# A gated recurrence and its feed-forward layer: 64-token chunks, k and b stacked, one solve pass, the feed-forward steps interleaved by a list scheduler

## The chip, the cores and the metric

One core of one Trainium2 chip runs the kernel, in one launch. The metric is device time in microseconds (us). A run that is over 1.5% above the fastest of its own kernel is called slow here, and only fast runs are compared. The engines have these names in the profile: PE is TensorE (matmul), PEld its weight load, DVE is VectorE, ACT is ScalarE, POOL is GpSimd, SP is SyncE, whose queue issues most of the DMAs (SPq). SBUF is the core's working memory; PSUM is the memory that TensorE writes its results to, in a few buffers.

## The reference

Four batches, eight heads, 768 tokens, 40 features a head. Each head carries a 40 x 40 state through the tokens; the result goes through a layer with squared relu.

```python
for t in range(S):                                   # 768 tokens
    y[:, :, t] = einsum('bhd,bhde->bhe', r_t, state) # read before the update
    Sa = einsum('bhde,bhe->bhd', state, a_t)
    state = state * w_t[:, :, None, :] - Sa (x) b_t + v_t (x) k_t
x = y.transpose(0, 2, 1, 3).reshape(3072, 320)
h = maximum(x @ w_in, 0)                             # 320 x 2048
out = (h * h) @ w_out                                # 2048 x 320, fp32
```

## The kernel before

It works in chunks of 128 tokens, six of them, for all 32 heads; a quad is four heads that lie in the same half of the array's rows. Decay is taken as cumulated logarithms (fp32 matmuls with a triangle of ones), k and b are divided by the decay and a and r multiplied by it. Then come triangular products within the chunk and products with the carried state. After all chunks the feed-forward layer (FFN) runs by itself.

```python
L = 128
# emit_prep, once per chunk: cumulated decay, fp32
cs = ps_prep_f32("cs")
nc.tensor.matmul(out=cs[:, 0:n], lhsT=UTI[:], rhs=lnW[:, s0:s1], start=True, stop=True)
# ... the same with UTE; the last row's decay spread to all rows, fp32 (rep)
rep = ps_prep_f32("rep")
nc.tensor.matmul(out=rep[:, 0:8 * D], lhsT=SEL127[:], rhs=GAM[:, c0:c0 + 8 * D], start=True, stop=True)
# ... transposes of R, V, K, A (bf16) and of the decay (fp32, trw)

# stage2, once per quad; stage1 has made the triangles Em and CmT
for i in range(4):
    nc.tensor.matmul(out=mstp[:, i, :], lhsT=AT[pb:pb + D, prs[i], :],      # 40 rows of the array
                     rhs=ST2[pb:pb + D, prs[i], :], start=True, stop=False)
    nc.tensor.matmul(out=mstp[:, i, :], lhsT=Em[:, i, :],                   # 128 rows
                     rhs=Vp[:, hhs[i], 0:D], start=False, stop=True)
# ...
for i in range(4):
    nc.tensor.matmul(out=xtp[:, i, :], lhsT=AT[pb:pb + D, prs[i], :],
                     rhs=Zb[pb:pb + D, i, :], start=True, stop=False)
    nc.tensor.matmul(out=xtp[:, i, :], lhsT=Em[:, i, :],
                     rhs=CmT[:, i, :], start=False, stop=True)
# ... yp (output), stp (state), stx (its transpose)

# after each chunk: 32 small copies by DMA that turn the heads' outputs into columns of x
nc.sync.dma_start(out=XTg[g][row0:row0 + D, tok0:tok0 + L], in_=YS[pb:pb + D, pr, :])

# after all chunks: the FFN
for j in range(16):                                    # in a loop over blocks tb of 512 tokens
    for g in range(3):
        nc.tensor.matmul(out=hp[:], lhsT=WIN[g][:, j * 128:(j + 1) * 128],
                         rhs=XTg[g][:, tb * 512:(tb + 1) * 512], start=(g == 0), stop=(g == 2))
    # ... copy to SBUF, max(x, 0) * x, then 16 matmuls of 320 columns with WOUT
```

Of the kernel before, what the change touches and what calls it, by code (L numbers as in the profile page):

```python
# [7 lines left out]
FP32 = mybir.dt.float32  # L9
BF16 = mybir.dt.bfloat16  # L10
ALU = mybir.AluOpType
ACTF = mybir.ActivationFunctionType


@with_exitstack
def kernel(
# [13 lines left out]

    NB, NHH, T, D = r.shape
    NH = NB * NHH
    L = 128
    NCH = T // L
    NP = NH // 2
    NQ = NH // 4
    DFF = moe_w_in.shape[1]
    DM = moe_w_in.shape[0]
    NTOK = NB * T

    gl = ctx.enter_context(tc.tile_pool(name="gl", bufs=1))

    ones_b = gl.tile([128, 128], BF16, name="ones_b")
    nc.vector.memset(ones_b[:], 1.0)
    IDb = gl.tile([128, 128], BF16, name="IDb")
    nc.gpsimd.affine_select(
        out=IDb[:], in_=ones_b[:], pattern=[[1, 128]],
        compare_op=ALU.is_equal, fill=0.0, base=0, channel_multiplier=-1,
    )
    MU4 = gl.tile([128, 4, 128], BF16, name="MU4")  # L50
    nc.vector.memset(MU4[:], 1.0)
    nc.gpsimd.affine_select(
        out=MU4[:], in_=MU4[:], pattern=[[0, 4], [1, 128]],
        compare_op=ALU.is_gt, fill=0.0, base=0, channel_multiplier=-1,
    )
    MUN4 = gl.tile([128, 4, 128], BF16, name="MUN4")
    nc.vector.memset(MUN4[:], -1.0)
    nc.gpsimd.affine_select(
        out=MUN4[:], in_=MUN4[:], pattern=[[0, 4], [1, 128]],
        compare_op=ALU.is_gt, fill=0.0, base=0, channel_multiplier=-1,  # L60
    )
    ones_f = gl.tile([128, 128], FP32, name="ones_f")
    nc.vector.memset(ones_f[:], 1.0)
    UTI = gl.tile([128, 128], FP32, name="UTI")
    nc.gpsimd.affine_select(
        out=UTI[:], in_=ones_f[:], pattern=[[1, 128]],
        compare_op=ALU.is_ge, fill=0.0, base=0, channel_multiplier=-1,
    )
    UTE = gl.tile([128, 128], FP32, name="UTE")
    nc.gpsimd.affine_select(  # L70
        out=UTE[:], in_=ones_f[:], pattern=[[1, 128]],
        compare_op=ALU.is_gt, fill=0.0, base=0, channel_multiplier=-1,
    )
    SEL127 = gl.tile([128, 128], FP32, name="SEL127")
    nc.gpsimd.affine_select(
        out=SEL127[:], in_=ones_f[:], pattern=[[0, 128]],
        compare_op=ALU.is_equal, fill=0.0, base=-127, channel_multiplier=1,
    )
    IDf = gl.tile([128, 128], FP32, name="IDf")
    nc.gpsimd.affine_select(  # L80
        out=IDf[:], in_=ones_f[:], pattern=[[1, 128]],
        compare_op=ALU.is_equal, fill=0.0, base=0, channel_multiplier=-1,
    )

    XTg = []
    for g in range(3):
        t_ = gl.tile([128, NTOK], BF16, name=f"XT{g}")
        nc.gpsimd.memset(t_[:], 0.0)
        XTg.append(t_)
    S2 = gl.tile([128, NP, D], BF16, name="S2")  # L90
    nc.gpsimd.memset(S2[:], 0.0)
    ST2 = gl.tile([128, NP, D], BF16, name="ST2")
    nc.gpsimd.memset(ST2[:], 0.0)
    GAMpad = gl.tile([128, NH, 64], FP32, name="GAMpad")
    nc.gpsimd.memset(GAMpad[:], 0.0)

    WIN = []
    gr_rows = [120, 120, 80]
    offw = 0
    for g in range(3):  # L100
        wt = gl.tile([128, DFF], BF16, name=f"WIN{g}")
        nc.gpsimd.memset(wt[:], 0.0)
        nc.gpsimd.dma_start(out=wt[0:gr_rows[g], :], in_=moe_w_in[offw:offw + gr_rows[g], :])
        WIN.append(wt)
        offw += gr_rows[g]
    WOUT = gl.tile([128, 16, DM], BF16, name="WOUT")
    nc.gpsimd.dma_start(out=WOUT[:], in_=moe_w_out.rearrange("(j p) f -> p j f", p=128))

    actx = ExitStack()
    actx.__enter__()  # L110
    natp = actx.enter_context(tc.tile_pool(name="natp", bufs=1))
    chp = actx.enter_context(tc.tile_pool(name="chp", bufs=2))
    qdp = actx.enter_context(tc.tile_pool(name="qdp", bufs=3))
    aps = actx.enter_context(tc.tile_pool(name="aps", bufs=1, space=bass.MemoryType.PSUM))

    def ps_prep_f32(name):
        return aps.tile([128, 512], FP32, name=name, tag="prep", bufs=2)

    def ps_prep_tr(name):
        return aps.tile([128, 1024], BF16, name=name, tag="prep", bufs=2)  # L120

    def chunk_view(src: bass.AP, c: int):
        return src[:, :, c * L:(c + 1) * L, :].rearrange("b h t e -> t (b h) e")

    nat_srcs = {"R": r, "K": k, "V": v, "W": w, "A": a, "B": b}

    def emit_dma(c):
        tiles_ = {}
        for key in ("R", "K", "V", "W", "A", "B"):
            t_ = natp.tile([128, NH, D], FP32, name=f"N{key}", tag=f"N{key}")  # L130
            nc.sync.dma_start(out=t_[:], in_=chunk_view(nat_srcs[key], c))  # L131
            tiles_[key] = t_
        return tiles_

    def emit_prep(c, nat):
        RN, KN, VN, WN, AN, BN = (nat[x] for x in ("R", "K", "V", "W", "A", "B"))
        o = {}
        Rp = chp.tile([128, NH, 64], BF16, name="Rp", tag="Rp", bufs=1)
        Vp = chp.tile([128, NH, 64], BF16, name="Vp", tag="Vp")
        Kp = chp.tile([128, NH, 64], BF16, name="Kp", tag="Kp")  # L140
        Ap = chp.tile([128, NH, 64], BF16, name="Ap", tag="Ap", bufs=1)
        for tt_ in (Rp, Vp, Kp, Ap):
            nc.gpsimd.memset(tt_[:, :, D:64], 0.0)  # L143
        o["Rp"], o["Vp"], o["Kp"], o["Ap"] = Rp, Vp, Kp, Ap
        nc.scalar.activation(out=Rp[:, :, 0:D], in_=RN[:], func=ACTF.Copy)  # L145
        nc.scalar.activation(out=Vp[:, :, 0:D], in_=VN[:], func=ACTF.Copy)
        lnW = chp.tile([128, NH * D], FP32, name="lnW", tag="lnW", bufs=1)
        nc.scalar.activation(out=lnW[:], in_=WN[:].rearrange("p h e -> p (h e)"),  # L148
                             func=ACTF.Ln)
        GAM = chp.tile([128, NH * D], FP32, name="GAM", tag="GAM", bufs=1)  # L150
        GAMP = chp.tile([128, NH * D], FP32, name="GAMP", tag="GAMP", bufs=1)
        blocks = [(0, 512), (512, 1024), (1024, NH * D)]
        GAMI = chp.tile([128, NH * D], FP32, name="GAMI", tag="GAMI", bufs=1)
        for (s0, s1) in blocks:
            n = s1 - s0
            cs = ps_prep_f32("cs")
            nc.tensor.matmul(out=cs[:, 0:n], lhsT=UTI[:], rhs=lnW[:, s0:s1],  # L157
                             start=True, stop=True)
            nc.scalar.activation(out=GAM[:, s0:s1], in_=cs[:, 0:n], func=ACTF.Exp)
            nc.scalar.activation(out=GAMI[:, s0:s1], in_=cs[:, 0:n], func=ACTF.Exp,  # L160
                                 scale=-1.0)
        for (s0, s1) in blocks:
            n = s1 - s0
            cs2 = ps_prep_f32("cs2")
            nc.tensor.matmul(out=cs2[:, 0:n], lhsT=UTE[:], rhs=lnW[:, s0:s1],
                             start=True, stop=True)
            nc.scalar.activation(out=GAMP[:, s0:s1], in_=cs2[:, 0:n], func=ACTF.Exp)
        GAMv = GAM[:].rearrange("p (h e) -> p h e", e=D)
        GAMIv = GAMI[:].rearrange("p (h e) -> p h e", e=D)
        GAMPv = GAMP[:].rearrange("p (h e) -> p h e", e=D)  # L170
        nc.scalar.activation(out=GAMpad[:, :, 0:D], in_=GAMv, func=ACTF.Copy)
        nc.vector.tensor_tensor(out=Kp[:, :, 0:D], in0=KN[:], in1=GAMIv, op=ALU.mult)  # L172
        Btn = chp.tile([128, NH, D], BF16, name="Btn", tag="Btn")
        nc.vector.tensor_tensor(out=Btn[:], in0=BN[:], in1=GAMIv, op=ALU.mult)
        nc.vector.tensor_tensor(out=Ap[:, :, 0:D], in0=AN[:], in1=GAMPv, op=ALU.mult)  # L175
        o["Btn"] = Btn
        GL2 = chp.tile([128, NP, D], BF16, name="GL2", tag="GL2")
        for blk in range(4):
            c0 = blk * 8 * D
            rep = ps_prep_f32("rep")  # L180
            nc.tensor.matmul(out=rep[:, 0:8 * D], lhsT=SEL127[:], rhs=GAM[:, c0:c0 + 8 * D],  # L181
                             start=True, stop=True)
            repv = rep[:, 0:8 * D].rearrange("p (pr s e) -> p pr s e", s=2, e=D)
            nc.vector.tensor_copy(
                out=GL2[0:64, blk * 4:(blk + 1) * 4, :],
                in_=repv[0:64, :, 0:1, :].rearrange("p a s e -> p a (s e)"))
            nc.vector.tensor_copy(  # L187
# [224 lines left out]
```

## Time and profile before

| | before |
|---|---|
| device time, median of 3 | 551.25 us (547.0 to 552.19) |
| loading, until TensorE works steadily | 43 us |
| the recurrence, 6 chunks | 385 us, 64 us each |
| the FFN | 122 us |

The page of the profile of before: busy time of each engine with its share of the span, the granted TensorE clock in 40 slices of the span (9 is full, 5 is half), and the chain of waits that ended last; then two groups of instructions (busy time, mean ns of one).

```profile
PE 500.9 (91%) x3570; PEld 304.5 (55%) x3576; DVE 292.6 (53%) x478; ACT 230.4 (42%) x403; POOL 49.3 (9%) x54
...
PEclk9957566856559558595668755796555799999999
...
PE 86%; DMA 5%; SPq 3%; ACT 2%; DVE 2%; issue 1%; ACTq 0%; DVEq 0%
...
L157 PE MATMUL cs<-lnW,UTI 128*128 128x512 f32 (+1 forms) x36 | 30.9, 972 | 18.7 <-ACT lnW L148 18.7
...
L181 PE MATMUL rep<-GAM,SEL_74 128*128 128x320 f32 x48 | 25.8, 666 | 14.6 <-DVE GL_166 L187 14.2
```

TensorE is both the busiest engine and 86% of the last chain, so it bounds the kernel. But the clock says that it is not working well: in most slices of the recurrence it is granted five or six tenths. The windows view of before gives the two stages apart (busy us of each engine, then the granted clock, the DMA share and GB/s):

```profile
core 0: us, PE busy (x) PEld busy (x) DVE busy (x) ACT busy (x) POOL busy (x), PEclk, DMA share, GB/s
43.00:428.00 385.00, 375.57 (x2890) 234.47 (x2891) 223.24 (x371) 149.91 (x267) 23.24 (x25) 0.66 0.37 54
428.00:550.00 122.00, 115.80 (x664) 65.83 (x668) 62.46 (x96) 67.59 (x120) 0.00 (x0) 0.98 0.10 34
```

In the recurrence TensorE is occupied for 98% of the time, at a granted clock of 0.66; in the FFN at 0.98. The timeline of before (start, duration, engine, line, operation, output <- inputs, array rows*columns, shape) shows how a busy TensorE can do little. Read the differences of the start times, since durations of pipelined matmuls overlap:

```profile
300.20 0.22 PE L290 MATMUL yp_3229<-CmT,Kp 128*40 128x128 bf16 x1
300.26 0.22 PE L292 MATMUL yp_3229<-XmT,Btn 128*40 128x128 bf16 x1
...
301.97 0.19 PE L274 MATMUL mstp_3207<-ST_86,AT 40*128 40x40 bf16 x1
302.09 0.19 PE L276 MATMUL mstp_3207<-Vp,Em 128*128 128x40 bf16 x1
302.22 0.19 PE L274 MATMUL mstp_3207<-ST_86,AT 40*128 40x40 bf16 x1
```

Matmuls of 128 columns that use the array in one shape start every 56 ns or so. Matmuls of only 40 columns that alternate between 40 and 128 array rows start every 120 to 130 ns. Elsewhere in this trace matmuls of 40 columns that keep one shape (stp, L304 and L306) start 25 ns apart at full clock, so it is the change of shape, not the work, that sets the pace.

### The profile page before, as it was taken

The numbers are of one execution on the slowest core, as the hardware profiler recorded it, in microseconds if no ns is written. First come the engines' busy times: TensorE is split into PE (matmuls) and PEld (weight loads), VectorE is DVE, ScalarE is ACT, GpSimd is POOL, SyncE is SP. The second block draws the span as 40 slices with busy tenths as digits, with TensorE's granted clock in tenths as the row PEclk, the third lists the DMA queues.
The fourth block names the chain that finished last, engine by engine and source line by source line (L and its number), as shares of the span: only waits on it lengthen the run. The fifth ranks groups of instructions, "written<-read, shape, count | busy, mean of one in ns | idle before, by whom it ended". The sixth has DMA issues, their size and how long they took to land.

```text
span 550.1 us, 8764 instructions
## 1 busy us (share of the span) xinstructions
PE 500.9 (91%) x3570; PEld 304.5 (55%) x3576; DVE 292.6 (53%) x478; ACT 230.4 (42%) x403; POOL 49.3 (9%) x54
## 2 busy tenths in 40 slices
PE   0609999999999999999999999999999799999997
PEld 0207546655667545765557665576666365566554
DVE  0126448634566446755467553775655536634752
ACT  1705542644125532255324325352112446744762
POOL 9903000011000200002001010000000000000000
PEclk9957566856559558595668755796555799999999
DMA  9999335633327330934108291000000010011011
GB/s 159 189 186 180 53 54 80 76 53 51 53 49 109 54 51 8 146 56 82 27 7 117 39 128 26 6 6 8 7 7 10 4 49 17 33 48 37 19 42 50
DMA packets 163577, 32.69 MB, mean 59 GB/s; under 512 B 158096, under 2 KB 163216, under 8 KB 163536
## 3 DMA queue, kind: packets, MB, share of 16 engines
q1 hardware_dynamic: 161088, 29.50, 34.5%
q0 software_dynamic: 2448, 2.62, 2.8%
q8 instruction: 28, 0.46, 0.4%
q14 instruction: 13, 0.11, 0.1%
HBM read 28.84 MB, written 3.93 MB: 60 GB/s over the span
## 4 chain that ended last, share of the span: by engine, by line
PE 86%; DMA 5%; SPq 3%; ACT 2%; DVE 2%; issue 1%; ACTq 0%; DVEq 0%
PE hp L360 11%; PE trp L198 5%; PE cs L157 5%; PE rep L181 4%; DMA NB<-in_b_dram 4%; SPq L131 3%; PE trw L213 2%; ACT Zb L271 1%; ACT AT L204 1%; DVE Ap L175 1%; PE op_5950 L374 0%; PE op_5910 L374 0%; PE op_5717 L374 0%; PE op_5544 L374 0%; PE op_5371 L374 0%
## 5 line engine op out<-in xcount | busy, mean ns | idle before, releaser
L367 DVE SCALAR_TENSOR_TENSOR Gt<-hsb 128x512 bf16<-128x512 bf16 x96 | 62.5, 692 | 49.6 <-ACT hsb L366 49.6
L366 ACT ACTIVATE hsb<-hp 128x512 bf16<-128x512 f32 x96 | 57.1, 597 | 12.3 <-DMA XT_82<-YS 5.5
L157 PE MATMUL cs<-lnW,UTI 128*128 128x512 f32 (+1 forms) x36 | 30.9, 972 | 18.7 <-ACT lnW L148 18.7
L374 PEld LDWEIGHTS <-Gt 128*128 128x128 bf16 x384 | 37.6, 98 | 15.5
L181 PE MATMUL rep<-GAM,SEL_74 128*128 128x320 f32 x48 | 25.8, 666 | 14.6 <-DVE GL_166 L187 14.2
L360 PE MATMUL hp<-XT_80,WIN_93 128*128 128x512 bf16 x96 | 37.5, 391 | 0.5 <-issue 0.2
L360 PE MATMUL hp<-XT_78,WIN_90 128*128 128x512 bf16 x90 | 35.0, 389 | 3.0 <-ACT hsb L366 2.4
L360 PE MATMUL hp<-XT_82,WIN_96 128*128 128x512 bf16 x96 | 37.6, 392 | 0.0
L297 DVE TENSOR_TENSOR YS<-ytmp,GT 40x512 bf16<-40x512 f32 x48 | 32.7, 681 | 0.5
L274 PEld LDWEIGHTS <-AT 40*128 40x128 bf16 x192 | 19.0, 99 | 20.1 <-issue 13.1
L292 PEld LDWEIGHTS <-Btn 128*40 128x40 bf16 x192 | 24.0, 130 | 11.0 <-issue 9.2
L284 PEld LDWEIGHTS <-Em 128*128 128x128 bf16 x192 | 19.3, 101 | 19.4 <-issue 2.1
L282 PEld LDWEIGHTS <-AT 40*128 40x128 bf16 x192 | 18.7, 98 | 19.1 <-issue 4.7
L290 PEld LDWEIGHTS <-Kp 128*40 128x40 bf16 x192 | 23.6, 123 | 4.1 <-issue 2.2
L276 PEld LDWEIGHTS <-Em 128*128 128x128 bf16 x192 | 19.5, 101 | 10.1 <-issue 2.8
L145 ACT ACTIVATE Rp<-NR 128x1280 bf16<-128x1280 f32 x6 | 7.6, 1269 | 40.7 <-PE trp L198 30.6
L181 PEld LDWEIGHTS rep<-GAM,SEL_74 128*128 128x128 f32 x48 | 11.5, 273 | 19.6 <-issue 17.0
L172 DVE TENSOR_TENSOR Kp<-NK,GAMI 128x1280 bf16<-128x1280 f32 x6 | 8.9, 1488 | 24.3 <-ACT GAMI L160 24.3
L157 PEld LDWEIGHTS cs<-lnW,UTI 128*128 128x128 f32 x36 | 9.1, 306 | 22.8 <-issue 20.8
L143 POOL MEMSET Rp<- 128x768 bf16 x6 | 4.5, 745 | 179.4 <-PE trp L198 179.4
L304 PEld LDWEIGHTS <-Vp 128*40 128x40 bf16 x192 | 15.1, 110 | 9.4 <-issue 7.3
L267 PEld LDWEIGHTS <-S_84 40*40 40x40 bf16 x192 | 14.9, 115 | 9.4 <-issue 6.0
(1138 smaller groups left out, 1074.1 us busy)
## 6 DMA issues: line engine op xcount, KB each, us to landing
NR<-in_r_dram SPq DMA_DIRECT2D x6, 640.0 KB
NK<-in_k_dram SPq DMA_DIRECT2D x6, 640.0 KB
NV<-in_v_dram SPq DMA_DIRECT2D x6, 640.0 KB
NW<-in_w_dram SPq DMA_DIRECT2D x6, 640.0 KB
NA<-in_a_dram SPq DMA_DIRECT2D x6, 640.0 KB
NB<-in_b_dram SPq DMA_DIRECT2D x6, 640.0 KB
out_dram<-osb SPq DMA_DIRECT2D x24, 160.0 KB
WOUT<-in_moe_w_out_dram POOLq DMA_DIRECT2D x1, 1280.0 KB, 14.5
```

The costliest lines, as they stand in the source:

```text
L157: nc.tensor.matmul(out=cs[:, 0:n], lhsT=UTI[:], rhs=lnW[:, s0:s1], start=True, stop=True)
L181: nc.tensor.matmul(out=rep[:, 0:8 * D], lhsT=SEL127[:], rhs=GAM[:, c0:c0 + 8 * D], start=True, stop=True)
L198: nc.tensor.transpose(out=trp[:, j * L:(j + 1) * L], in_=srcv, identity=IDb[:])
L276: nc.tensor.matmul(out=mstp[:, i, :], lhsT=Em[:, i, :], rhs=Vp[:, hhs[i], 0:D], start=False, stop=True)
L284: nc.tensor.matmul(out=xtp[:, i, :], lhsT=Em[:, i, :], rhs=CmT[:, i, :], start=False, stop=True)
L290: nc.tensor.matmul(out=yp[pb:pb + D, i, :], lhsT=Kp[:, hhs[i], 0:D], rhs=CmT[:, i, :], start=(i == 0), stop=False)
L292: nc.tensor.matmul(out=yp[pb:pb + D, i, :], lhsT=Btn[:, hhs[i], 0:D], rhs=XmT[:, i, :], start=False, stop=(i == 3))
L297: nc.vector.tensor_tensor(out=YS[pb:pb + D, pc:pc + 4, :], in0=ytmp[pb:pb + D, :, :], in1=GT[pb:pb + D, pc:pc + 4, 0:L], op=ALU.mult,)
L360: nc.tensor.matmul(out=hp[:], lhsT=WIN[g][:, j * 128:(j + 1) * 128], rhs=XTg[g][:, tb * 512:(tb + 1) * 512], start=(g == 0), stop=(g == 2),)
L366: nc.scalar.activation(out=hsb[:], in_=hp[:], func=ACTF.Copy)
L367: nc.vector.scalar_tensor_tensor(out=Gt[:, j, :], in0=hsb[:], scalar=0.0, in1=hsb[:], op0=ALU.max, op1=ALU.mult,)
L374: nc.tensor.matmul(out=op_[:], lhsT=Gt[:, j, s_ * 128:(s_ + 1) * 128], rhs=WOUT[:, j, :], start=(j == 0), stop=(j == 15),)
```

## The change

The intent: halve the work that grows with the square of the chunk, keep TensorE on full-rate bf16 work in few array shapes, and mix the FFN's dense matmuls with the recurrence's small ones.

- Chunks of 64 tokens, two batches on the two halves of the partitions: 24 groups (12 chunks x 2 batch pairs).
- k and b lie in opposite halves of one tile, so one triangle and one set of transposes serve both. The inner solve is one correction pass (UA, UB, then COR).
- fp32 matmuls become pairs of bf16 matmuls (high and low half of the logarithm); the copies of the outputs by DMA become transposes on TensorE.
- The FFN of a group runs among the next groups' recurrence steps.
- Every step is an entry with an engine, an assumed duration, an array shape and a place; a list scheduler in the kernel's Python puts them in order. The order is fixed when the kernel is built.
- The FFN weights are loaded whole at the start, behind eight POOL memsets.

The diff replaces nearly the whole body; its core, cut:

```diff
-    L = 128
+    L = 64
+    NG = NCH * (NB // 2)
+PERIOD = 9.3
+PLACE = {"LW": -40, ..., "KT": -8, ..., "X0": 0, ..., "U0": 9, ..., "D3": 15.5, "OE": 16, "OST": 16.5}
+SWITCH = 0.1
+RINGS = {"S": 3, "D": 1, "HP": 1, "F": 1}            # PSUM buffers by class
+class Plan:
+    def run(self):
+        ...
+                    if e == "PE" and mode != o.mode:
+                        t += SWITCH
+        ...
+                d = 0.2 if e == "PE" else 0.05
+                t, o = min((x for x in lst if x[0] <= t0 + d),
+                           key=lambda x: (x[1].place + (1.5 if e == "PE" and x[1].mode != mode else 0), x[1].seq))
+        ...
+            if e == "SP":
+                nd, xfer = o.dur
+                free[e] = t + nd * 0.34              # assumed time to issue one copy
+    ...
+    for t in LNW + LLO + A + RB:
+        nc.gpsimd.memset(t[:], 0.0)
+    ...
+        def halves(dst, off, src, other):            # one copy per batch: two per tensor
+            for be in range(2):
+                h = 1 - be if other else be
+                nc.sync.dma_start(out=V(dst, off(be), [(40, 8), (1, 40)], 64 * h, 64), in_=tok(src, b0 + be))
+        add("LW", g, "SP", (2, 1.1), lambda: halves(wf, lambda be: 0, w, False), [("LN", g - NL)])
+        # ... LK, LB, LA, LV the same; LR one copy: 11 in and 2 out per group
+    ...
+                    for al in range(2):              # state: the two column halves alternate
+                        mm(out=V(p, 40 * i, [(1, 40)], 64 * al, 64), lhsT=V(kb, 128 * i + 64 * al, [(1, 64)]), ...)
+    ...
+    order = plan.run()
+    load_weights()
+    for o in order:
+        o.fn()
```

## The prediction

> **What bounds it now.** TensorE. The busy table gives PE 91%, DVE 53%, ACT 42%, POOL 9%; the chain of waits is 86% PE. Three parts: 43 us of loading, the recurrence to 428 us (64 us per 128-token chunk), the FFN, 122 us. The windows view grants 0.66 of the clock in the recurrence, 0.98 in the FFN. In the recurrence TensorE is occupied but inefficient: by start gaps in the timeline, 128-column matmuls of one array shape come every 56 ns at full clock, 107 at half; the alternation AT(40 rows)/Em(128 rows) costs 160 and 218 ns per matmul. Those pairs (xtp, mstp) take about 100 us; fp32 matmuls (cs, rep, trw) 71 us.
>
> **What changes.** fp32 matmuls go (high/low bf16 halves instead); GL replication, GAMpad transposes, XT copies by DMA and 12 ACT table loads (1.28 us each) go. Chunk 64 halves the quadratic work; pairs of heads use two halves of the array at once; K and B are stacked, so one triangle serves both. The FFN is interleaved.
>
> Work per group (24 of 2 x 64 tokens), from the trace's durations:
> - PE at full clock: FFN 16 x 136 ns (320 columns) + 32 x 56 + 16 half-row at 28 = 4.4 us; 31 transposes x 56 = 1.7 us; small tiles 3 us (estimate from 25 ns for a 40-column matmul in one tile, about half with two). Sum 9.1 us. The instruction order has 12.3 changes of array shape per group; at the 105 ns (160 - 56) that one costs in the trace, 1.3 us more: 10.4 us. The Trainium skill, TensorEngine Tiling, Key Properties, says that a change of mode drains the engine; the 105 ns agrees.
> - DVE about 8.0 us (0.69 us per 512 fp32 PSUM columns, 0.69 per 1024 bf16), ACT 6.7 us (0.60 per 512 columns), POOL about 6 us (a guess: not in this trace), DMA about 5.5 us (a 4096-packet load took 3.56 us).
>
> So PE still bounds it, the rest 50 to 77% busy. Static order, one triangle buffer and one FFN output buffer cost gaps: I take 5 to 8% idle PE, period 11.0 us. 24 x 11.0 = 264, plus about 22 us until TensorE is dense (memsets, loads, first chain, cold clock) and 9 us for the last group's chain: **295 us**, range 272 to 330.
>
> **Clock.** By the Trainium skill, TensorE: Matmul & The Clock Gate, the clock is halved after a 3.4 us window of little activity.[...] A new group streams 19,300 columns, 8.0 us at full clock, 0.73 of 11 us, its FFN steps spread: it should stay warm after the start.
>
> **Chances.** Faster by over 2%: 0.985; within: 0.01; slower: 0.005.
>
> **What would show it.** Right: clock over 0.9 between 40 and 270 us; PE the chain's largest share; period 10.5 to 11.5 us (spacing of output stores); DVE 70 to 78% busy; 40-column tile pairs at 13 to 15 ns per matmul; DMA share near 40%. Wrong: clock below 0.8 mid-run; PE waiting on POOL (KB, A, VM) or DVE (EBM, CPM) over 15%; small-tile gaps of 25 ns and more (1.5 us per group, 36 us).
>
> **What would make it wrong.** Half clock in mid-run (+60 us); column halves not running together (+36 us); POOL much slower than guessed beside a busy DVE; weights arriving after 35 us.

## The result, and the profile after

| | before | after |
|---|---|---|
| device time, median of 4 | 551.72 us (547.0 to 554.28) | 317.53 us (315.07 to 317.98) |
| ratio of the fast runs | | 0.5757, 95% interval 0.5719 to 0.5795 |
| TensorE busy | 500.9 us | 271.5 us |
| granted clock, whole run, as the profile has it (too high after, see below) | 0.74 to 0.76 | 0.97 to 0.99 |

A ratio here is the mean time of one kernel's fast runs over that of the other's of the same rounds, so it isn't quite the ratio of the two medians quoted. The result is right on the reference.

The page after; its lines answer to those of before, with the busy tenths of TensorE and of the DMA engines in the 40 slices added:

```profile
PE 271.5 (86%) x5928; PEld 216.9 (69%) x5928; DVE 186.9 (59%) x288; ACT 149.6 (47%) x265; POOL 142.4 (45%) x259
...
PE   0132899599999899999999999999999999999872
...
PEclk9999999989999799999999999999999999999999
DMA  5999776677665766666665765657564311001110
...
PE 70%; SPq 11%; DVE 6%; ACT 5%; DMA 3%; issue 3%; POOL 0%; ACTq 0%; POOLq 0%
```

The time fell by 234 us and TensorE's busy time by 229 us. From 48 us on the clock is near full. SPq, the queue that issues the copies, is now 11% of the chain, and the slices say where: TensorE is nearly empty in the first four, while the DMA engines are full from the second on. The windows view after:

```profile
core 0: us, PE busy (x) PEld busy (x) DVE busy (x) ACT busy (x) POOL busy (x), PEclk, DMA share, GB/s
0.00:20.00 20.00, 4.33 (x42) 2.87 (x42) 11.18 (x30) 2.90 (x4) 13.64 (x31) 1.00 0.88 149
20.00:40.00 20.00, 10.18 (x160) 7.55 (x158) 5.40 (x7) 5.00 (x11) 7.83 (x15) 1.00 0.95 149
40.00:80.00 40.00, 36.38 (x755) 29.77 (x752) 22.05 (x33) 19.39 (x34) 19.79 (x37) 0.96 0.70 120
120.00:280.00 160.00, 156.62 (x3663) 126.90 (x3661) 107.14 (x159) 87.73 (x157) 77.45 (x140) 1.00 0.52 94
280.00:316.00 36.00, 25.93 (x501) 20.62 (x499) 16.31 (x24) 13.24 (x21) 1.49 (x2) 0.98 0.09 20
```

TensorE works 14.5 us of the first 40, then 91% and later 98% of the time. The pace is read from the copy that takes each group's result out of PSUM; the first five in the timeline after:

```profile
59.66 0.42 ACT L593 ACTIVATE OSB<-fo 128x320 f32<-128x320 f32 x1
70.83 0.44 ACT L593 ACTIVATE OSB<-fo 128x320 f32<-128x320 f32 x1 [1.25 <-PE fo L588]
81.76 0.44 ACT L593 ACTIVATE OSB<-fo 128x320 f32<-128x320 f32 x1 [2.01 <-PE fo L588]
92.75 0.44 ACT L593 ACTIVATE OSB<-fo 128x320 f32<-128x320 f32 x1 [1.04 <-PE fo L588]
108.83 0.44 ACT L593 ACTIVATE OSB<-fo 128x320 f32<-128x320 f32 x1 [3.02 <-PE fo L588]
```

The first result is out at 60.1 us, the last at 312.1: 23 gaps of 10.96 us in the mean, with one of 16.1 and three short ones at the end. The steady pace is the predicted 11.0 us. What is late is the first result. A piece of TensorE's timeline in steady state shows that the pace is made as predicted (x16 is sixteen matmuls, 128*64 a column half of the array):

```profile
201.28 0.43 PE L481 MATMUL st<-VM,KB 128*64 128x40 bf16 x16
201.55 0.36 PE L486 MATMUL st<-I,SB 128*40 128x40 bf16 x16
201.84 0.41 PE L429 MATMUL eb<-ART,KBT 40*128 40x64 bf16 x16
202.09 0.39 PE L561 MATMUL hp<-XT,WIN 64*128 64x128 bf16 x8
...
207.22 0.41 PE L525 MATMUL y<-KB,CPM 128*64 128x40 bf16 x16
207.48 0.31 PE L533 MATMUL y<-SB,ART 128*64 128x80 bf16 x8
```

Sixteen matmuls of 40 columns in two alternating column halves take 0.27 us from the first start to the next step's, 16 to 17 ns each in the mean. The Trainium skill, TensorE: Matmul & The Clock Gate, Part 1, says that the spacing never drops below about 25 ns however few the columns. The trace agrees for one tile: 25 ns before, and here about 32 ns from one matmul to the next in the same half. It is the two halves of a pair that start only 3 to 4 ns apart, so the mean over both is lower. Summing TensorE's start gaps from 120 to 280 us by kind, per group of about 10.9 us: 7.9 us inside steps, 0.7 from a step to the next of the same shape (54 ns each), 1.8 at changes of shape (174 in this stretch, 154 ns each in the mean) and 0.5 waiting, 4.6%. The first three make 10.4 us, which is the predicted sum of work and changes of shape. (How large the parts are depends on where a gap is counted as a wait; e12's expectation below starts from 0.7 us of waits.)

Now the start. The timeline after, first 28 us (the queue's records are the time that the queue was held by the issue, not the transfer; the Trainium skill, Perfetto Trace Analysis, DMA Instruction — HWDGE, says that the record ends when the sequencer is free for the next instruction, and that the moving of the data isn't in it; here the data of the line at 8.73, whose record ends at 16.44, were used at 27.05):

```profile
1.73 3.98 DVE L198 COPY TI<-UI 64x64 bf16<-64x64 bf16 x1 [0.56 <-POOL UI L183]
1.89 0.97 POOL L237 MEMSET LNW<- 128x512 f32 x2
...
5.62 1.29 POOL L247 DMA_DIRECT2D WIN<-in_moe_w_in_dram  x2
...
8.73 7.71 SPq L289 DMA_DIRECT2D Wf<-in_w_dram  x2
...
27.05 0.47 ACT L307 ACTIVATE LNW<-Wf 128x320 f32<-128x320 f32 x1 [10.95 <-DMA Wf<-in_w_dram]
```

Three suspects stand in it. (A) The weights, 2.88 MB, go out at 5.6 to 8.6 us and the second group's loads, issued at 8.7, sit behind them. (B) The queue: in the stretch after 60 us, where the DMA engines aren't full, two copies of 80 KB take 1.27 to 1.30 us to issue, where the scheduler assumed 0.34 for each. (C) The setup: a 64x64 copy on VectorE takes 3.98 us beside POOL's memsets.

```profile
60.91 1.27 SPq L289 DMA_DIRECT2D Wf<-in_w_dram  x2
...
71.16 0.58 SPq L302 DMA_DIRECT2D Rf<-in_r_dram  x1
```

Ten copies at 0.64, one at 0.58 and two output stores at 0.59 us are 8.2 us of queue time per group of 10.96; the queue issues nearly back to back until about 110 us to build up the loads' lead.

One more thing is in the start that the clock's view hides. The profile has no clock record of this run before 48.1 us, and the view counts such time as full. The spacing of the matmuls says that it was half. Timeline after:

```profile
18.14 1.06 PE L384 MATMUL kt<-ID,KB 128*128 128x128 bf16 x8
...
48.12 0.61 PE L384 MATMUL kt<-ID,KB 128*128 128x128 bf16 x8
```

The same eight transposes of 128 columns start 107 ns apart up to 48.02 us and 56 ns apart from 48.17 us on. So the 1.00 of the first two rows of the windows view is not measured, and TensorE was at half clock from the first of these transposes, at 17.8 us, on. From 32 to 48.1 us it was occupied for 14.6 of 16.1 us, so there the half clock cost time: 7 us by halving, or 4 if only the 7.9 us after 40 us count (estimates). In e1, e2 and e4 below the first clock record, at full, comes at 26.7, 42.2 and 37.2 us, so what these runs gain in the start contains what an earlier full clock gains; the two were not separated.

### The profile page after: what moved, and what is told of

Its sections match the earlier page's. It is cut to its first block, busy times and chain, and to the rows that moved or that the text cites. A ratio compares the mean times of both kernels' runs of the same rounds, so it can differ in the third digit from the quotient of the medians.

```text
span 315.7 us, 13625 instructions
## 1 busy us (share of the span) xinstructions
PE 271.5 (86%) x5928; PEld 216.9 (69%) x5928; DVE 186.9 (59%) x288; ACT 149.6 (47%) x265; POOL 142.4 (45%) x259
## 3 DMA queue, kind: packets, MB, share of 16 engines
q1 hardware_dynamic: 134016, 27.55, 49.5%
q0 software_dynamic: 2496, 2.88, 5.5%
## 4 chain that ended last, share of the span: by engine, by line
PE 70%; SPq 11%; DVE 6%; ACT 5%; DMA 3%; issue 3%; POOL 0%; ACTq 0%; POOLq 0%
PE fo L588 17%; PE hp L570 15%; SPq L289 10%; PE hp L561 5%; PE sx L500 3%; PE vt L511 3%; PE kt L384 3%; PE rt L401 3%; DVE GT L579 3%; PE cs L323 2%; PE y L525 2%; ACT RL L575 2%; DMA Wf<-in_w_dram 2%; PE st L481 2%; PE x L444 2%
## 5 line engine op out<-in xcount | busy, mean ns | idle before, releaser
L575 ACT ACTIVATE RL<-hp 128x1024 bf16<-128x1024 f32 x48 | 49.1, 1023 | 63.7 <-PE hp L570 60.8
L588 PE MATMUL fo<-WOUT,GT 128*128 128x320 bf16 x384 | 61.5, 303 | 3.5 <-DVE GT L579 3.1
L356 POOL TENSOR_TENSOR KB<-KBf,EXN 128x320 bf16<-128x320 f32 x48 | 40.8, 870 | 35.6 <-issue 12.3
L570 PE MATMUL hp<-XT,WIN 128*128 128x128 bf16 x768 | 54.4, 223 | 0.0
L570 PEld LDWEIGHTS <-WIN 128*128 128x128 bf16 x768 | 45.4, 100 | 5.6 <-issue 0.4
L588 PEld LDWEIGHTS <-GT 128*128 128x128 bf16 x384 | 34.8, 99 | 17.3 <-DVE GT L579 5.1
L579 DVE TENSOR_TENSOR GT<-RL 128x1024 bf16<-128x1024 bf16 x48 | 37.7, 785 | 12.5 <-ACT RL L575 12.2
L372 POOL CAST VM<-Vf 64x320 bf16<-64x320 f32 x48 | 23.2, 483 | 27.1 <-issue 15.5
L433 DVE TENSOR_TENSOR CPM<-cp,MASK 128x1024 bf16<-128x1024 f32 x24 | 29.2, 1216 | 4.5 <-PE cp L429 4.5
L433 DVE TENSOR_TENSOR EBM<-eb,MASK 128x1024 bf16<-128x1024 f32 x24 | 29.2, 1217 | 3.2 <-PE eb L429 3.1
L329 ACT ACTIVATE EXN<-cs 128x640 f32<-128x640 f32 x24 | 16.8, 700 | 14.6 <-PE cs L323 13.9
L367 POOL CAST RB<-Rf 128x320 bf16<-128x320 f32 x24 | 11.3, 470 | 27.0 <-PE rt L401 11.5
L315 POOL TENSOR_TENSOR LLO<-LNW 128x320 bf16<-128x320 f32 x24 | 17.8, 742 | 9.1 <-ACT LNW L307 8.4
L593 ACT ACTIVATE OSB<-fo 128x320 f32<-128x320 f32 x24 | 10.5, 436 | 22.2 <-PE fo L588 22.1
L307 ACT ACTIVATE LNW<-Wf 128x320 f32<-128x320 f32 x24 | 11.2, 466 | 20.1 <-DMA Wf<-in_w_dram 20.0
```

Source lines behind the costliest of these rows:

```text
L356: nc.gpsimd.tensor_tensor(out=V(kb, 512 * be, [(64, 8), (1, 40)]), in0=V(kbf, 320 * be, [(40, 8), (1, 40)]), in1=V(exn, 320 * be, [(40, 8) ...
L372: nc.gpsimd.tensor_copy(out=V(vm, 512 * be, [(64, 8), (1, 40)], h, 64), in_=V(vf, 0, [(40, 8), (1, 40)], h, 64))
L433: nc.vector.tensor_tensor(out=V(dst, 0, [(64, 16), (1, 64)]), in0=V(psum(key, g), 0, [(64, 16), (1, 64)]), in1=V(MASK, 0, [(0, 16), (1, 64 ...
L570: mm(out=V(p, 512 * s + 128 * i, [(1, 128)]), lhsT=WIN[x][:, 128 * blk:128 * blk + 128], rhs=xt[:, 128 * x:128 * x + 128], start=False, st ...
L575: nc.scalar.activation(out=rl[:], in_=psum(f"hp{hf}", g)[:], func=ACTF.Relu)
L579: nc.vector.tensor_tensor(out=gt[:], in0=rl[:], in1=rl[:], op=ALU.mult)
```

## The experiments

Twelve kernels were run, each an edit of the changed kernel, in three jobs on three chips. Each job ran the kernel before as well (medians 551.83, 552.57 and 551.99 us), so the ratios to it can be compared between jobs; the changed kernel's is 0.5757. The theories of the start are A (the weights' traffic), B (the issues), C (the setup on POOL and VectorE). Further ones concern the steady state: P (TensorE bounds, the rest has slack) and I (the gain needs the FFN in between).

### e1_no_weight_load

```diff
-    load_weights()
+    for t in WIN + [WOUT]:
+        nc.vector.memset(t[:], 0.0)
```

The result is wrong (the weights are zero). The steps themselves take the same time, as the later gaps below show.

> Wrong result on purpose: the FFN weights are zeroed by the idle VectorE and not loaded. The first output of the changed kernel came at 60 us, TensorE was dense only from about 43 us, not from 22 as predicted. Theory A (the weights' 17 us of all 16 DMA engines compete with the loads of the first three groups): first output at 46 to 50 us, time 303 to 307 us. Theory B (the issuing queue, 0.64 us per copy and 11 copies a group, holds the loads back): first output at 54 to 58 us, time 312 to 316. Theory C (set-up work on POOL and VectorE holds the first chain back): no change, 316 to 318.

Measured: 303.07 us, ratio 0.5479 [0.5447, 0.5510]. The first result is out at 45.5 us instead of 60.1, and the later gaps are the same as after (11.2, 10.9, 11.0, 16.4). The windows view of this run:

```profile
20.00:40.00 20.00, 18.54 (x381) 14.72 (x375) 12.43 (x18) 11.18 (x22) 16.10 (x29) 1.00 0.70 123
```

TensorE works 18.5 of these 20 us where it worked 10.2. The packets in the two traces show what was in the way: from 8 to 20 us SyncE's queue moved 113 packets per us after and 723 in e1, while the weights' packets took 0.89 of the DMA engines' time after. So A is shown: the weights' load at the start costs 14.5 us (medians; a full clock that comes 21 us later is part of that), though the FFN is not what waits for it.

### e2_one_issue

```diff
+        def whole(dst, off, src):
+            t0 = min(c * L, T - 2 * L)
+            x = src[b0, :, t0:t0 + 2 * L, :].rearrange("h t e -> t h e")
+            nc.sync.dma_start(out=V(dst, off, [(40, 8), (1, 40)]), in_=x)
-        add("LW", g, "SP", (2, 1.1), lambda: halves(wf, lambda be: 0, w, False), [("LN", g - NL)])
+        add("LW", g, "SP", (2, 1.1), lambda: whole(wf, 0, w), [("LN", g - NL)])
         # ... LK, LB, LA and LV the same
```

Its output is wrong, which doesn't matter for the time. One copy of 128 tokens of one batch takes the place of two copies of 64 tokens of two batches. The bytes are the same, the issues 8 per group instead of 13.

> Wrong result on purpose: each of W, K, B, A, V of a group is fetched by one copy of 128 partitions instead of two of 64, same bytes, same number of 160-byte pieces, same order of everything else; 8 copies are issued per group instead of 13. Theory B: the issuing queue is busy 5.3 us per group instead of 8.5 to 8.8, the loads of groups 2 to 8 land earlier, first output at 50 to 55 us, the 16 us output gap near 100 us goes, time 300 to 308 us. Theory A: first output within 3 us of 60, time 312 to 317. Theory C: no change.

Measured: 305.15 us, ratio 0.5529 [0.5507, 0.5551]. First result at 51.5 us, the gap of 16.1 became 13.9. Windows view of this run:

```profile
20.00:40.00 20.00, 13.23 (x226) 9.96 (x222) 6.96 (x9) 6.83 (x15) 8.88 (x17) 1.00 1.11 181
40.00:80.00 40.00, 39.96 (x892) 32.36 (x888) 25.66 (x40) 23.07 (x42) 25.50 (x43) 1.00 0.88 162
```

With fewer issues the DMA engines move 181 GB/s from 20 to 40 us instead of 149, and TensorE is full from 40 us on. The packets themselves are hardly faster: by the pages' DMA sections they took 49.5% of 315.7 us of 16 engines for 134,016 packets after, 18.7 ns each, and 49.2% of 303.4 us for 132,096 in e2, 18.1 ns each. So the gain is of the fewer issues rather than of a faster transfer. So B holds as well, for 12 us. A and B act on the same stretch, so their two gains must not be added; how they split was not measured.

### e3_setup_order

```diff
     for t in LNW + LLO + A + RB:
-        nc.gpsimd.memset(t[:], 0.0)
+        nc.vector.memset(t[:], 0.0)
-            add(f"VZ{be}", g, "POOL", 0.4, f, [("VT", g - 3), ("ST", g - 3)])
+            if g >= 3:
+                add(f"VZ{be}", g, "POOL", 0.4, f, [("VT", g - 3), ("ST", g - 3)])
```

> Right result. The eight POOL memsets go to VectorE, behind its small copies of the masks, and the zeroing of VM that is done twice for the first three groups is left out, so POOL's first LLO no longer waits to 13.6 us. Theory C: the first chain starts 4 to 6 us earlier, first output at 54 to 56 us, time 311 to 314 us. Theories A and B: first group's own chain earlier, but the second group's loads bound the start all the same, time 315 to 318. In all theories the small mask copies take 0.2 us each instead of 2 us mean, if POOL's memsets were what held them.

Measured: 315.0 us, ratio 0.5709 [0.5683, 0.5734], correct. The intervals of the two ratios overlap (0.5719 to 0.5795 after), so at most a small gain. The timeline of this run shows why:

```profile
1.72 0.25 DVE L198 COPY TI<-UI 64x64 bf16<-64x64 bf16 x1 [0.56 <-POOL UI L183]
1.89 1.29 POOL L247 DMA_DIRECT2D WIN<-in_moe_w_in_dram  x2
...
18.77 0.86 POOL L356 TENSOR_TENSOR KB<-KBf,EXN 128x320 bf16<-128x320 f32 x1 [12.23 <-DMA KBf<-in_b_dram]
```

The setup itself was cured: the copy takes 0.25 us instead of 3.98. But the weights now go out at 1.9 us instead of 5.6, ahead of more of the first group's loads, and POOL waits 12.2 us for b. The wait only changed its name. C alone is refuted as a cause of much.

### e4_scheduler_cost

```diff
-                free[e] = t + nd * 0.34
-                dma_free = max(dma_free, t + nd * 0.34) + xfer
+                free[e] = t + nd * 0.64
+                dma_free = max(dma_free, t + nd * 0.64) + xfer
```

Nothing of the work changes, only the order: the scheduler is told the measured issue time.

> Right result. Only the scheduler's own assumption is changed: 0.64 us per copy issued (measured 0.60 to 0.66) instead of 0.34. Theory B, with order at fault: steps are put in an order that fits the true arrival of the loads, PE waits between 30 and 110 us shrink by 3 to 8 us, time 309 to 314. Theory B with the queue alone at fault, and A and C: within 2 us of 317.

Measured: 310.71 us, ratio 0.5634 [0.5607, 0.5661], correct. First result at 52.0 us, then a gap of 16.3. So 6.8 us of the miss came from an order that was worked out with half the true cost of an issue.

### e5_ffn_after

```diff
+for _n in PLACE:
+    if _n[:2] in ("U0", "U1", "UX", "UY", "RL", "SQ", "D0", "D1", "D2", "D3", "OE", "OS"):
+        PLACE[_n] += 1000
-    XT = ring("XT", 2, 384)
+    XT = ring("XT", NG, 384)
     # ... XTE no longer waits for the FFN steps of group g - 2
-            add(f"U{hf}", g, "PE", 0.24, f, [("XTE", g)], mode="R", ...)
+            add(f"U{hf}", g, "PE", 0.24, f, [("XTE", g), ("XTE", NG - 1)], mode="R", ...)
```

The same steps, but every FFN step waits for the end of the whole recurrence, as in the kernel before.

> Right result. One part of the change undone: the FFN steps wait until the last group's recurrence is through, in the same scheduler, all else kept. Theory I (interleaving fills TensorE where the recurrence alone would be limited by VectorE, 6.4 us a group, and by the issue of copies, 8.5 us a group): recurrence alone at 8.5 to 9.5 us a group, TensorE 60 to 75% busy there, maybe at half clock in part, then an FFN stage of 110 to 125 us: 350 to 385 us. Rival (TensorE is the limit in either order, its work is the same): 317 to 330 us.

Measured: 425.68 us, ratio 0.7708 [0.7646, 0.7769], correct. The size was missed: 350 to 385 us was expected. The windows view of this run, once in each stage:

```profile
40.00:240.00 200.00, 158.38 (x4153) 129.59 (x4147) 132.80 (x199) 84.56 (x178) 115.59 (x214) 0.88 0.61 106
280.00:400.00 120.00, 82.49 (x1065) 66.16 (x1063) 22.85 (x33) 41.97 (x51) 0.00 (x0) 1.00 0.10 23
```

Alone, the recurrence takes 8.8 us per group (4153 matmuls in 200 us, 183 a group), with TensorE busy 79% of the time at a recorded clock of 0.88; some of its waits are for the loads of w, which the faster pace outruns. The FFN takes 7.2 us per group (1065 in 120 us, 64 a group) with TensorE at 69%: its one PSUM buffer (HP) makes TensorE wait for ScalarE at every half, 36.7 us in the second window. That buffer was sized for a kernel in which other work fills the wait. Together 16.0 us, against 10.96 interleaved: 108 us for the whole run. Some of that is the missing buffer. With the pace of the FFN in the kernel before, 122 us / 24 = 5.1 us per group, the sum would be 13.9 us and interleaving worth about 24 x (13.9 - 10.96) = 71 us; this is an estimate. The direction supports I, and both numbers say that the interleaving is a large part of the gain.

### e6_no_timing

```diff
-        while left:
-            ...                       # earliest start by assumed durations, lags and switches
+        while avail:
+            for o in sorted(avail, key=lambda o: (o.place, o.seq)):
+                ...                   # the first by place whose PSUM buffer is free
```

The same steps and places; the order no longer knows durations.

> Right result. The scheduler's times are taken away: steps are put in order by their place value alone, with dependences and buffers kept; the order has 16.6 changes of array shape per group instead of 12.3. Theory S (the timing in the scheduler matters): 4.3 x 0.105 us x 24 = 11 us for the changes and 5 to 20 us of waits more, 330 to 350 us. Rival (the skew of the place values does it all): within 2%, 311 to 324 us.

Measured: 482.16 us, ratio 0.8747 [0.8696, 0.8798], correct. The expectation of 330 to 350 us was far off. A result comes every 18.7 us, all the time, at a clock of 0.87. The waits of this run from 120 to 400 us (us in total, times, longest):

```profile
POOL KB L316 <- ACT EXN L289: 141.7, 15, 9.7
...
PE eb L389 <- DVE CPM L393: 38.8, 15, 2.6
```

Fifteen groups end in this window, and every one makes TensorE wait 2.6 us for VectorE to free the only triangle buffer and POOL 9.4 us for the decay. Order by place alone lines the steps of one group up behind one another. So the timed order is worth 165 us here: more than any other part of the change that was taken away singly.

### e7_tensor_more

```diff
-            for i in range(8):
+            for i in list(range(8)) * 2:
                 nc.tensor.transpose(out=p[:, 128 * i:128 * i + 128], in_=kb[:, 128 * i:128 * i + 128], identity=ID[:])
```

> Right result. Eight transposes of KB per group are done twice, 8 x 56 ns = 0.45 us of TensorE per group that the scheduler isn't told of. Theory P (TensorE bounds the steady state): +0.45 x 24 = 10.8 us, 327 to 330 us. Rival (a chain through the other engines bounds it): under +4 us.

Measured: 322.28 us, ratio 0.5850 [0.5809, 0.5891], correct: 4.8 us more for 0.45 us of extra TensorE work in each of the 24 groups (10.8 us). The mean gap between results rose by 0.19 us. It lies between the two expectations, so TensorE isn't a pure bound. Presumably the extra work in part fills waits that were there; which ones was not traced.

### e8_vector_more

```diff
-        add("EBE", g, "DVE", 1.22, lambda: masked("eb", ebm), ...)
+        add("EBE", g, "DVE", 1.22, lambda: (masked("eb", ebm), masked("eb", ebm)), ...)
```

> Right result. The masking of one triangle (EBM, 1.22 us on VectorE) is done twice per group, which the scheduler isn't told of: VectorE goes from 7.8 to 9.0 us of a 10.9 us group. Theory P (TensorE bounds, VectorE has slack): under +8 us, up to 325. Rival (VectorE, or the chain through it, bounds as well): +1.22 x 24 = 29 us, 340 to 348.

Measured: 334.66 us, ratio 0.6066 [0.6031, 0.6101], correct: 17.1 us more for 1.22 us of extra VectorE work per group (29 us). The mean gap rose by 0.72 us. The chain of waits of this run:

```profile
PE 46%; DVE 30%; SPq 12%; issue 3%; DMA 3%; ACT 3%; POOL 2%; POOLq 0%; DVEq 0%; ACTq 0%
```

VectorE's share of the chain was 6% after. An engine that is 67% busy in steady state should have absorbed this if it had slack. It is a fixed order, and the lengthened step was not announced to the scheduler, so what stands behind it waits: TensorE's waits between steps from 120 to 280 us rose from 7.3 to 19.0 us. They are waits for this one step: 7.7 us by the next triangle (cp), which needs the only triangle buffer, and 4.1 us by the product (x) that uses the masked triangle. P is only partly right: TensorE is the largest limit, but the fixed order couples it to VectorE, and idle time on VectorE is not the same as slack.

### e9_spread_weights

```diff
-    load_weights()
+    loads = [(lambda i=i, n=n: load_win(i, n)) for n in range(4) for i in range(3)]
+    loads += [(lambda n=n: load_wout(n)) for n in range(4)]
+    for i, f in enumerate(loads):      # 16 pieces, paced 2.2 us apart in the plan
+        add(f"WT{i}", 0, "POOL", 0.6, f, [("LN", 0)] if i == 0 else [(f"WT{i - 1}", 0)])
     # ... group 0's FFN steps are told to wait for their pieces
```

> Right result. The FFN weights are loaded in 16 pieces that are issued between POOL's steps of the first five groups instead of in four at the start; nothing else is changed but what the scheduler is told of them. Theory A: most of the 14.5 us that went with the weights in e1 comes back, first output at 48 to 53 us, time 304 to 310. If only their sheer volume counts (DMA engines full either way): first output at 57 to 60, time 314 to 318.

Measured: 310.14 us median of all four runs, of which one was slow (the fast ones 308.7, 308.77 and 311.5), ratio 0.5619 [0.5581, 0.5657], correct. The time is near what was expected, the way to it was not: the first result comes at 61.1 us, no earlier than after, but the second follows at 64.5 instead of 71.3. The recurrence of the later groups got ahead, while the first group's FFN waited for its weights: its last three products with WOUT start at 53.2, 56.6 and 59.9 us, each as its piece lands.

### e10_spread_setup_cost

The edits of e9, e3 and e4 together.

```diff
+    # e9: the weights in 16 paced pieces
+    # e3: the four memsets on VectorE, VZ only for g >= 3
-                free[e] = t + nd * 0.34
+                free[e] = t + nd * 0.64
```

> Right result. e9, with the set-up of e3 and the issue cost of e4 together. In e3 the weights were issued 3.7 us earlier and held B's first load back to 21 us; with them spread, theory C has its chance: first chain 6 us earlier than in e9. Expected first output at 42 to 47 us, time 296 to 302. If the gains are not additive (the second group's loads bound it): 301 to 306.

Measured: 308.36 us, ratio 0.5596 [0.5568, 0.5625], correct: the lowest ratio of a correct version, 0.5596 / 0.5757 = 0.972 of the changed kernel, though its interval overlaps those of e9 and e4. It missed both of its expected ranges, upwards. Timeline and windows view of this run:

```profile
50.73 0.74 POOL L253 DMA_DIRECT2D WOUT<-in_moe_w_out_dram  x1
53.94 0.78 POOL L253 DMA_DIRECT2D WOUT<-in_moe_w_out_dram  x1
```

```profile
20.00:40.00 20.00, 15.43 (x232) 11.93 (x231) 7.63 (x12) 7.76 (x15) 12.69 (x25) 0.74 0.93 145
40.00:80.00 40.00, 33.28 (x694) 26.43 (x694) 20.29 (x30) 15.98 (x30) 20.18 (x37) 0.91 0.87 144
```

The last two pieces of WOUT were issued at 50.7 and 53.9 us, where 16 pieces at a pace of 2.2 us from the first (1.90 us) would have ended by 35. The pieces stand in POOL's stream in order, and POOL's own steps before them wait for other engines. The granted clock of 0.74 from 20 to 40 us is no loss against after: this run's clock records begin at 25.0 us, and after was at half clock all through that stretch. The first result came at 63.2 us.

### e11_second_queue

```diff
+        E = "ACT" if g < 1 else "SP"
-        add("LA", g, "SP", (2, 1.1), ...)
+        add("LA", g, E, D2, ...)        # LV the same: group 0's loads of a and v from ScalarE's queue
```

On top of e10.

> Right result. e10, with A and V of the first group issued by ScalarE's queue, so that the second group's loads are issued 2.6 us earlier. If issue (theory B) still bounds the start: 2 to 4 us less than e10. If not: within 1.5 us of e10.

Measured: 314.19 us median, correct; two of four runs were slow and the fast ones took 312.59 and 310.51 us, so it isn't better than e10. The Trainium skill, Trainium Kernel Development and Optimization, Key Constraints, says that issuing from several engines saves only the sequencer's issue time; this run can't test that, but the DMA engines' share was 0.86 from 0 to 20 us and 0.96 from 20 to 40, so there was little room for a second queue.

### e12_fewer_shapes

```diff
-                d = 0.2 if e == "PE" else 0.05
+                d = 0.8 if e == "PE" else 0.05
-                           key=lambda x: (x[1].place + (1.5 if e == "PE" and x[1].mode != mode else 0), x[1].seq))
+                           key=lambda x: (x[1].place + (8.0 if e == "PE" and x[1].mode != mode else 0), x[1].seq))
```

The order is made to prefer a step of the current array shape: 8.3 changes of shape per group instead of 12.3.

> Right result. On the changed kernel, the scheduler is made to prefer the array shape in use (bonus 8 instead of 1.5, search window 0.8 us instead of 0.2): 8.3 changes of shape per group instead of 12.3. If the 0.105 us per change were saved without new waits: 4 x 0.105 x 24 = 10 us, 307 us. Rival (the longer runs of one shape hold other steps back, and waits take the gain): 315 to 335 us, PE waits per group up from 0.7 us.

Measured: 352.09 us, ratio 0.6389 [0.6359, 0.6419], correct: 34.6 us slower. At the 100 ns that a change adds (154 - 54), four fewer changes should have saved 0.4 us per group. Instead TensorE's waits between steps from 120 to 280 us rose from 7.3 to 18.3 us, mostly behind VectorE's masks and state and, for 4.7 us, ScalarE's relu, and the gaps between results alternate between 10.2 and 14 to 15 us. Delaying a step to save a change of shape delays what waits for it on the other engines.

## Why the prediction was right or wrong

Predicted 295 us (272 to 330), measured 317.53: inside the range, faster as expected, and 22.5 us over the centre.

**The sum, term by term.** "24 x 11.0 = 264": measured 24 x 10.96 = 263. "about 22 us until TensorE is dense ... and 9 us for the last group's chain", together 31: measured 315.7 - 263.1 = 52.6 us. The device time is 1.7 us longer than the profiled span. So 21.6 us of the miss lie in start and end, 1.7 in what the span leaves out, and -0.9 in the steady part. The end was near its 9 us: TensorE is idle 10 us of the last 36. The step that failed is "about 22 us until TensorE is dense (memsets, loads, first chain, cold clock)"; by this sum it measures 42 to 44. The windows view confirms it: 957 matmuls were started by 80 us, which at the steady 3663 per 160 us are 42 us of work, so TensorE was 38 us behind by then, and the gap of 16.1 us near 100 us adds some 4 more. It was not empty all that time: it worked 7.8 of the first 32 us, and then 14.6 of the 16.1 to 48.1 at half clock.

**Why the start was mis-sized.** The prediction counted what the first group needs, not what else was in its way. Shown: the weights' load costs 14.5 us (e1), the number of issues 12 us (e2), the order worked out with an issue cost of 0.34 us instead of about 0.64 costs 6.8 us (e4). These overlap, and each may contain a part of what the half clock costs; the prediction had named the cold clock in its 22 us, but it lasted to 48.1 us. Setup alone is worth at most some 2.5 us (e3), because the loads were the next wait. Among the causes of failure, the prediction listed "weights arriving after 35 us". They arrived by 26.7 us and the FFN didn't wait for them; they did harm by arriving early, ahead of the second group's loads.

**The steady state, right for the reasons given.** TensorE is the chain's largest share (70%). The granted clock is 0.96 to 1.00 from 80 to 280 us; from 40 to 80 the view's 0.96 leaves out the half clock up to 48.1, and over all of 40 to 270 us it is 0.97, over the predicted 0.9. After 48.1 us two stretches at half clock are left, at 61.8 and 106.1 us, of 3.41 us each, which agrees with the 3.4 us window that the prediction took from the skill. The period is 10.96 us (10.5 to 11.5 predicted). Pairs of tiles in column halves take 16 to 17 ns per matmul in four steps of 40 columns and 12 in the fifth (13 to 15 predicted, so missed a little on both sides). Waits between steps are 4.6% (5 to 8 predicted). That POOL was no limit rests on a figure that the prediction called a guess, 6 us per group; it is 5.3 in steady state (77.45 us of 160), which was luck. The Trainium skill's statement that a change of mode drains the array (TensorEngine Tiling, Key Properties) fits: a step starts 154 ns after the last matmul of another shape against 54 after one of the same, 100 ns more, where the prediction took 105 from the trace before for each of 12.3 changes per group.

**Off in size.** DMA share: near 40% was predicted; the windows show 0.70 from 40 to 80 us and 0.52 from 120 to 280 (the prediction's own 5.5 us of 11 would have been 0.50). The estimate of 5.5 us of all DMA engines per group came from one large load's record; measured, the queue's packets took 49.5% of 315.7 us, 6.5 us per group. VectorE was 67% busy against 70 to 78.

**Where the gain lies.** Before, a group's share is 385 / 24 = 16.0 us of recurrence and 5.1 us of FFN. The new recurrence alone takes 8.8 us (e5), so the new algorithm in its timed order saves 7.2 us per group, and the interleaving saves 2.9 more (estimate) up to 5.0 (with e5's own FFN). The order by time is what makes both possible: without it the same steps take 482 us (e6). "So PE still bounds it" was right as a ranking, but e8 shows that VectorE's step on the way costs 0.72 us of period for 1.22 us of work, which a single bound would not.

**Left open.** How A, B and the half clock divide the start; how short it could be with weights paced by something other than POOL's own stream; whether e11's second queue helps in undisturbed runs; what causes the one gap of 16 us (it shrank in e2 and e3, moved in e4; between 96 and 110 us ScalarE waits 2.0 us for a load of w, but no single wait was shown to be it); and how much each of the smaller chunk, the stacking and the bf16 halves gives, since they were not taken apart.

## What to carry to other kernels

When the middle of a kernel has become short, count the start as its own stage: every load that is in flight before the first dense work, how many issues it takes at the measured time per issue, and which bulk loads can wait. Check a view of the clock against the spacing of equal matmuls, since time without a record can pass for full clock. A fixed order made by a scheduler is only as good as its durations, so put the measured ones in; and measure slack by lengthening a step, because in a fixed order an engine's idle share doesn't show it. Saving array-shape changes, or any other local cost, pays only if what waits for the moved step on other engines has time.

## What the Trainium skill lacked or had wrong

- TensorE: Matmul & The Clock Gate, Part 1, gives a floor of about 25 ns between matmul starts without saying that it is for one tile (the same page's part on packing has tiles start a few ns apart). Two alternating column halves ran at 16 to 17 ns per matmul of 40 columns here (st and y steps, 201.28 to 201.55 us and 207.22 to 207.48 us): 3 to 4 ns between the halves, about 32 within one.
- The same page, Back-to-back issue gap, gives about 81 ns for a sustained stream of weight load and matmul at 128 columns. Such pairs ran at 56 ns per matmul here at full clock (1.07 us recorded for 16 in the hp step, 0.90 from its start to the next step's).
- TensorEngine Tiling, Key Properties, gives no size for the drain at a change of mode. Here a matmul in an alternation of shapes cost 160 ns against 56 (before), and a step started 154 ns in the mean after the last matmul of another shape, 54 ns after one of the same (after).
- SBUF — State Buffer, Who interferes with whom, says that a copy on VectorE, in a mode that uses two ports, and a GpSimd instruction block each other for the whole instruction. Here two 64x64 copies took 3.98 and 3.83 us, until the last of eight POOL memsets was over, so the wait was for a row of instructions, not for one; with the memsets elsewhere they took 0.25 and 0.16 us. Which mode the copies ran in the trace doesn't show.
- DMA: Bandwidth & Descriptors has no measured time for issuing a copy from the SP queue on this chip (its part on trn3 has a vendor's cycle count for earlier generations). Here it was 0.58 to 0.66 us per copy of 80 or 160 KB, so 13 copies took 8.2 us of a group's 10.96.
